# A fused mLSTM and two feed-forward layers: dense column sums on TensorE, and the first group's clipping on ScalarE

## The chip, the core and the metric

The kernel runs on one core of one Trainium2 chip. The metric is the device time of one execution in microseconds, lower is better. A core has five engines with a queue of instructions each, which run beside one another and wait for each other by semaphores: TensorE (PE; matmuls into PSUM, PEld its weight loads), VectorE (DVE), ScalarE (ACT), GpSimd (POOL) and SyncE (SP), which here issues most DMAs. Each engine takes its instructions strictly in the order in which they were written, so an instruction that waits holds up everything behind it on its engine.

## The reference

Three layers follow each other. An mLSTM attention over 4 batches, 8 heads and 768 steps gives 3072 tokens of 320 features. A dense feed-forward layer with 2048 hidden features follows, and then a routed one with 8 experts. The middle layer is the one that the change touches:

```python
def _moe_ref(x, w_in, w_out):                 # x: 3072 x 320, w_in: 320 x 2048, w_out: 2048 x 320
    h = x @ w_in
    g = np.where(h >= 1, h, np.where(h <= -1, 0.0, (h + 1) ** 2 / 4))
    return g @ w_out

def _moe2_ref(x, w_gate, w1, w2):             # shortened
    logits = x @ w_gate                       # 8 experts, each takes 384 tokens, best logits first
    ...
    out[mask] = np.maximum(x[mask] @ w1[e], 0) @ w2[e]
```

## The kernel before

**Tiling.** The 3072 tokens make 8 groups of 384 (three chunks of 128). For each group the dense layer runs over 16 feature tiles of 128 hidden features. One feature tile is an up step (`ff_up`, line 783: 8 matmuls of 384 columns into one PSUM tile `ph`), an activation, and a down step (`ff_down`, line 845: 3 matmuls of 328 columns for each of three chunks into `po`). Every 32-bit factor is split into a high part in the format `fp32r` and a low part, the rest, so an up step has high times high, high times low and low times high products, and a down step three. The 328 columns are the 320 of `w_out` and 8 more, `w_out` times the gate weights, so that the routed layer's logits come out of the same matmuls.

**The activation.** On the scaled up result, ScalarE makes `u = relu(h/2 + 1/2)` (line 793) and `r = relu(h - 1)` (line 795), VectorE clips `u` to at most 1 (line 797), ScalarE squares it (line 798), VectorE forms `r - 0.25 + u` (line 799), ScalarE writes its high part `gh` (line 810) and VectorE its low part `gl` (line 811). What comes out is g - 0.25, not g. So 0.25 times the column sums of `w_out` has to be added to every down result: that row is `crow`. GpSimd adds up the 16 weight tiles in `crow`, one add of 128 x 328 for each (line 753); then `col_sums` multiplies it by a 128 x 128 tile full of 0.25 (`quart`), which sums over the partitions and gives the same row to each of them (line 757), and ScalarE writes it back (line 759). Lines 834 and 865 add it.

**The weights.** In group 0 the weights of the 16 feature tiles come in as 64-bit numbers and are decoded (`load_w`): one step on ScalarE (line 714), three on VectorE (lines 716, 717 and 719, all in the buffer `ws`), then high parts on ScalarE (lines 725 and 748) and low parts on GpSimd (726 and 750). TensorE transposes the tile (`pw`, line 733) and multiplies it by the gate weights (`pg`, line 744). So up step f of group 0 needs decoded tile f. Groups 1 to 7 use the same weights from SBUF.

**Attention beside it.** While the dense layer of group g runs, the attention chunks of group g + 1 are worked on between its steps: loads, a scan (line 489), scores (`ps`, lines 558 and 562), state (`pu`, `um`, lines 576 and 579), outputs (`py`, lines 597 to 624), and the split of the result into `xh` and `xl` (lines 638 to 646). Their PSUM tiles come from a pool `psa` of three.

**What sets the order.** All steps are given to a planner (`Plan`) with an estimated duration, the tiles read and written, and a due time, which runs backwards from the steps that need them. `order` places the steps one by one: on each engine, of those that could start at the earliest time, the one due first. `issue` writes the instructions in that order. Where TensorE has an early gap, filler matmuls on `quart` stand in it (`pdm`, line 347). The planner's estimates only set the order; on the chip every engine runs through its queue as its semaphores allow.

## Time and profile before

| | us |
|---|---|
| median of 3 runs (lowest, highest) | 859.82 (858.64, 862.1) |
| the profiled execution's own time | 859.59 |
| its span, first to last instruction | 857.9 |
| TensorE busy (share of the span) | 804.5 (94%) |
| VectorE busy | 636.1 (74%) |
| ScalarE busy | 460.6 (54%) |
| GpSimd busy | 246.7 (29%) |

The shares are means over stages. Group 0 of the dense layer begins with its first up step at 53.20 us and ends near 158 us, groups 1 to 7 follow, and behind them the routing and the experts. Three views are used below. The view by stage has for each stretch its length and the busy time of PE, PEld, DVE, ACT and POOL with the count of instructions, then the granted clock of TensorE (1.00 is full), the DMA engines' busy share and GB/s. The view of waits names an instruction and what ended its engine's idle time before it. The timeline has a start, a duration and an instruction, written as line, operation and out<-in by the names in the program. Matmuls are pipelined, so the durations of neighbours overlap; how fast they run is read from one start to the next.

### The profile page before, as it was taken

The page shows a single profiled execution, that of the slowest core. Times are in us where ns is not written, and L with a number is a line of the kernel's source. Part 1 is how long each engine was busy: PE and PEld are TensorE (multiplying, and loading weights), DVE is VectorE, ACT ScalarE, POOL GpSimd, SP SyncE. Part 2 cuts the span into 40 slices and gives each one's busy share as a digit, 9 for nine tenths or more (in the row PEclk, how much of TensorE's full clock was granted, in tenths as well). Part 3 has the DMA queues.
Part 4 walks back from the last instruction along what each step waited for, and adds up shares of the span by engine and source line. Part 5 has one row for each costly group of instructions (what it writes and reads, how often), then busy time and mean ns, then how long its engine had stood idle before and what let it go on. Part 6 is the DMA issues. An engine that isn't in the chain of part 4 may idle for free. (4 is left out here: it accounts for less than half of the span.)

```text
span 857.9 us, 15542 instructions
## 1 busy us (share of the span) xinstructions
PE 804.5 (94%) x5459; PEld 751.3 (88%) x5459; DVE 636.1 (74%) x1549; ACT 460.6 (54%) x986; POOL 246.7 (29%) x332
## 2 busy tenths in 40 slices
PE   9988898999999999999999999998979799999896
PEld 7877787899999999999999998887959598898896
DVE  6889978676886886877787666747667787897461
ACT  4456666757656657657566667902233433442551
POOL 4666756220221320120221235002030321322411
PEclk9998899999999999999999999999979699999999
DMA  9775554031432423441430000005042442452630
GB/s 198 195 194 142 144 149 97 24 76 45 97 68 57 94 64 70 96 98 22 105 70 16 24 2 24 1 8 160 26 156 59 139 143 89 133 159 79 202 106 24
DMA packets 167846, 78.36 MB, mean 91 GB/s; under 512 B 105432, under 2 KB 164056, under 8 KB 167768
## 3 DMA queue, kind: packets, MB, share of 16 engines
q1 hardware_dynamic: 165464, 69.50, 31.7%
q0 software_dynamic: 2304, 7.87, 2.8%
q8 instruction: 43, 0.70, 0.3%
q14 instruction: 35, 0.29, 0.1%
HBM read 69.28 MB, written 8.06 MB: 90 GB/s over the span
## 5 line engine op out<-in xcount | busy, mean ns | idle before, releaser
L783 PE MATMUL ph<-xh,wi 128*128 128x384 f32 x768 | 180.4, 345 | 0.6 <-ACT r L795 0.4
L845 PE MATMUL po<-wo,gh 128*128 128x328 f32 (+1 forms) x690 | 162.5, 319 | 0.8 <-ACT gh L810 0.4
L783 PEld LDWEIGHTS ph<-xh,wi 128*128 128x128 f32 x768 | 134.9, 191 | 3.0 <-ACT r L795 2.0
L845 PEld LDWEIGHTS po<-wo,gh 128*128 128x128 f32 x690 | 120.4, 192 | 2.9 <-ACT gh L810 2.3
L845 PE MATMUL po<-wo,gl 128*128 128x328 f32 (+1 forms) x345 | 109.8, 318 | 4.5 <-DVE gl L811 4.4
L799 DVE SCALAR_TENSOR_TENSOR r<-r,u 128x384 f32<-128x384 f32 x128 | 77.9, 609 | 34.1 <-ACT u L798 33.2
L783 PE MATMUL pf<-xh_e,w1t 128*128 128x384 f32 x384 | 98.8, 363 | 0.1
L793 ACT ACTIVATE u<-ph,half 128x384 f32<-128x384 f32 x128 | 74.2, 580 | 39.4 <-PE ph L783 38.6
L810 ACT ACTIVATE gh<-r 128x384 fp32r<-128x384 f32 x115 | 60.3, 524 | 64.6 <-DVE r L799 64.6
L1311 ACT ACTIVATE hh<-pf 128x384 fp32r<-128x384 f32 x64 | 31.5, 492 | 114.2 <-PE pf L783 85.9
L811 DVE TENSOR_TENSOR gl<-r,gh 128x384 fp32r<-128x384 f32 x115 | 73.1, 636 | 25.0 <-ACT gh L810 24.3
L845 PE MATMUL pe<-w2t,hh 128*128 128x320 f32 x384 | 89.4, 319 | 0.0
L798 ACT ACTIVATE u<-u 128x384 f32<-128x384 f32 x128 | 67.3, 526 | 26.7 <-DVE u L797 26.0
L783 PE MATMUL ph<-xl,wi 128*128 128x384 f32 x256 | 76.2, 350 | 0.0
L795 ACT ACTIVATE r<-ph,none 128x384 f32<-128x384 f32 x128 | 74.4, 581 | 0.5 <-DVE st L811 0.5
L783 PEld LDWEIGHTS pf<-xh_e,w1t 128*128 128x128 f32 x384 | 71.2, 201 | 1.7 <-ACT xh_e L640 0.6
L845 PEld LDWEIGHTS po<-wo,gl 128*128 128x128 f32 x345 | 65.9, 191 | 6.6 <-DVE gl L811 6.6
L797 DVE TENSOR_SCALAR u<-u 128x384 f32<-128x384 f32 x128 | 54.4, 425 | 16.7 <-ACT u L793 15.8
L845 PEld LDWEIGHTS pe<-w2t,hh 128*128 128x128 f32 x384 | 65.3, 192 | 0.2
L845 PE MATMUL pe<-w2t,hl 128*128 128x320 f32 x192 | 59.8, 311 | 0.0
L1312 DVE SCALAR_TENSOR_TENSOR hl<-pf,hh 128x384 fp32r<-128x384 f32 x64 | 35.5, 555 | 28.6 <-ACT hh L1311 27.9
L489 DVE TENSOR_TENSOR_SCAN g<-g,identr 128x1024 f32<-128x1024 f32 x22 | 53.6, 2437 | 0.2
(219 smaller groups left out, 1634.3 us busy)
## 6 DMA issues: line engine op xcount, KB each, us to landing
g<-fz_d SPq DMA_DIRECT2D x22, 512.0 KB
r<-in_moe_w_dram SPq DMA_DIRECT2D x32, 320.0 KB
r<-in_moe_w_dram SPq DMA_DIRECT2D x32, 256.0 KB
raw<-in_moe_w_out_dram SPq DMA_DIRECT2D x16, 320.0 KB
raw<-in_moe_w_in_dram SPq DMA_DIRECT2D x16, 256.0 KB
r<-in_moe_w_dram SPq DMA_DIRECT2D x64, 64.0 KB
qn<-in_q_dram SPq DMA_DIRECT2D x24, 160.0 KB
kn<-in_k_dram SPq DMA_DIRECT2D x24, 160.0 KB
```

The costliest lines, as they stand in the source:

```text
L489: add("V", 2.25, lambda: V.tensor_tensor_scan(hl(gt()), hl(gt()), hl(identr()), 0.0, op0=OP.mult, op1=OP.add), r=[identr], w=[gt])
L783: T.matmul(ps()[:, :TG], wsrc(m, j), x()[:, j, :], start=(i == 0), stop=(i == len(ops) - 1))
L793: add("A", cost_act(TG, True), lambda: A.activation(u(), ps()[:, :TG], AF.Relu, bias=half(), scale=0.5 / 256), r=[ps, half], w=[u])
L795: add("A", cost_act(TG, True), lambda: A.activation(r(), ps()[:, :TG], AF.Relu, bias=none(), scale=1.0 / 256), r=[ps, none], w=[r])
L797: add("V", cost_v(TG, True), lambda: V.tensor_scalar(u(), u(), 1.0, None, op0=OP.min), w=[u])
L798: add("A", cost_act(TG, psum=False), lambda: A.activation(u(), u(), AF.Square), w=[u])
L799: add("V", cost_v(TG), lambda: V.scalar_tensor_tensor(r(), r(), -0.25, u(), op0=OP.add, op1=OP.add), r=[u], w=[r])
L810: add("A", cost_act(TG, psum=False), lambda: A.activation(hv(), r(), AF.Copy), r=[r], w=[hk])
L811: add("V", cost_v(TG), lambda: V.tensor_tensor(lv(), r(), hv().bitcast(F32), op=OP.subtract), r=[r, hk], w=[lk])
L845: T.matmul(po()[:, :n], a()[:, cs], w(), start=(first and m == 0), stop=(last and m == 2))
L1311: add("A", cost_act(TG), lambda ps=ps, hh=hh: A.activation(hh(), ps()[:, :TG], AF.Relu), r=[ps], w=[hh])
L1312: add("V", cost_v(TG), lambda ps=ps, hh=hh, hl=hl: V.scalar_tensor_tensor(hl(), ps()[:, :TG], 0.0, hh().bitcast(F32), op0=OP.max, op1=OP.s ...
```

## The change

Three edits. The 16 adds into `crow` on GpSimd go, and `col_sums` instead multiplies the tile of 0.25 (a copy `quart_r` in the format `fp32r`, made by VectorE) by the high and low parts of all 16 down weight tiles, 32 matmuls of 328 columns that accumulate in one PSUM tile of the pool `psa`; the planner gets them in 8 steps of four. In group 0 alone, the clipping of `u` on VectorE is replaced: ScalarE makes `relu(1 - u)` and then squares `1 - ` that, which is min(u, 1) squared. In the other groups the clipping stays.

```diff
--- before.py
+++ after.py
@@ -329,6 +329,7 @@
     none = ct([P, 1], F32, "none")
     crow = ct([P, DO], F32, "crow")
     quart = ct([P, P], F32R, "quart")
+    quart_r = ct([P, P], F32R, "quart_r")
     wg = ct([P, 3, NE], F32, "wg")
 
     def g_ident():
@@ -338,6 +339,7 @@
     add("G", 2.2, g_ident, w=[identr])
     if 20:
         add("V", 0.2, lambda: V.memset(quart().bitcast(F32), 0.25), w=[quart])
+        add("V", 0.16, lambda: V.tensor_copy(quart_r(), quart().bitcast(F32)), r=[quart], w=[quart_r])
         pdm = pl.tile(at(ps_o), [P, 512], F32, "pso", GC, "pdm")
 
         def filler(t):
@@ -403,8 +405,7 @@
         G.tensor_tensor(pair(), identr()[:2 * NE, 0, :NE], identr()[:2 * NE, 0, NE:2 * NE], op=OP.add)
         G.memset(half(), 0.5)
         G.memset(none(), -1.0)
-        G.memset(crow(), 0.0)
-    add("G", 1.4, g_small, r=[identr], w=[hm, half, none, crow, pair])
+    add("G", 1.4, g_small, r=[identr], w=[hm, half, none, pair])
 
     NR = 3
     KG = 2
@@ -750,12 +751,16 @@
         add("G", 1.2, lambda: G.tensor_tensor(
             w2_()[:, 1, f2, :], ws()[:, 3 * P:], w2_().bitcast(F32)[:, 0, f2, :], op=OP.subtract),
             r=[ws, (ws, "g"), (w2_, f, 0)], w=[(w2_, f, 1)])
-        add("G", 1.2, lambda: G.tensor_tensor(crow(), crow(), ws()[:, 3 * P:], op=OP.add), r=[ws, (ws, "g")], w=[crow])
 
     def col_sums():
         ps = pst("pcol")
-        add("T", 0.56, lambda: T.matmul(ps()[:, :DO], quart().bitcast(F32), crow(), start=True, stop=True),
-            r=[quart, crow], w=[ps])
+        for lo in range(0, NF, 2):
+            def f(lo=lo):
+                for f in (lo, lo + 1):
+                    for m in range(2):
+                        T.matmul(ps()[:, :DO], quart_r(), wo(f)()[:, m, f % (NF // 2), :],
+                                 start=(f == 0 and m == 0), stop=(f == NF - 1 and m == 1))
+            add("T", 4 * (DO * 0.000445 + 0.003), f, r=[quart_r] + wo_k(lo) + wo_k(lo + 1), w=[ps])
         add("A", cost_act(DO), lambda: A.activation(crow(), ps()[:, :DO], AF.Copy, scale=1.0 / 256), r=[ps], w=[crow])
 
     def spare():
@@ -794,8 +799,12 @@
             r=[ps, half], w=[u])
         add("A", cost_act(TG, True), lambda: A.activation(r(), ps()[:, :TG], AF.Relu, bias=none(), scale=1.0 / 256),
             r=[ps, none], w=[r])
-        add("V", cost_v(TG, True), lambda: V.tensor_scalar(u(), u(), 1.0, None, op0=OP.min), w=[u])
-        add("A", cost_act(TG, psum=False), lambda: A.activation(u(), u(), AF.Square), w=[u])
+        if g == 0:
+            add("A", cost_act(TG, psum=False), lambda: A.activation(u(), u(), AF.Relu, bias=1.0, scale=-1.0), w=[u])
+            add("A", cost_act(TG, psum=False), lambda: A.activation(u(), u(), AF.Square, bias=1.0, scale=-1.0), w=[u])
+        else:
+            add("V", cost_v(TG, True), lambda: V.tensor_scalar(u(), u(), 1.0, None, op0=OP.min), w=[u])
+            add("A", cost_act(TG, psum=False), lambda: A.activation(u(), u(), AF.Square), w=[u])
         add("V", cost_v(TG), lambda: V.scalar_tensor_tensor(r(), r(), -0.25, u(), op0=OP.add, op1=OP.add), r=[u], w=[r])
         k = f - (NF - ND) - 3
         if g < NG - 1 or k < 0:
```

The planner orders group 0 anew; from the fourth up step of group 1 on, every engine has the same instructions in the same order as before. Three places of the new order, on TensorE and VectorE. The first is TensorE's queue around up step 9 of group 0 (`ph_9`), before:

```order
L733 MATMUL pw_1257<-identr,ws_1175 128x128 x2
L733 MATMUL pw_1257<-identr,ws_1175 64x128
L499 MATMUL pq_1266<-identr,qn_94 120x128 x3
L845 MATMUL po_0_696<-wo_1076,gh_8_1252 128x328 x2
L845 MATMUL po_0_696<-wo_1076,gl_8_1255 128x328
L845 MATMUL po_1_702<-wo_1076,gh_8_1252 128x328 x2
L845 MATMUL po_1_702<-wo_1076,gl_8_1255 128x328
L845 MATMUL po_2_737<-wo_1076,gh_8_1252 128x328 x2
L845 MATMUL po_2_737<-wo_1076,gl_8_1255 128x328
L744 MATMUL pg_1290<-wg,wt_1270 128x8 x3
L783 MATMUL ph_9_1296<-xh_403,wi_1018 128x384 x3
```

and now (`pw` and `pg` are the transposed weight tile and its gate product, `pu` and `ps` belong to an attention chunk, `po` is a down step):

```order
L734 MATMUL pw_1261<-identr,ws_1185 128x128 x2
L734 MATMUL pw_1261<-identr,ws_1185 64x128
L577 MATMUL pu_1268<-v_0_117,kn_112 120x126 x3
L761 MATMUL pcol<-wo_425,quart_r 128x328 x4
L559 MATMUL ps_0_1285<-qm_1137,kT_1220 128x384
L761 MATMUL pcol<-wo_425,quart_r 128x328 x4
L745 MATMUL pg_1296<-wg,wt_1288 128x8 x3
L788 MATMUL ph_9_1301<-xh_403,wi_1042 128x384 x3
L788 MATMUL ph_9_1301<-xl_431,wi_1042 128x384 x2
L788 MATMUL ph_9_1301<-xh_403,wi_1042 128x384 x3
L639 MATMUL px_1319<-identr,x_615 128x128 x3
L854 MATMUL po_0_695<-wo_1074,gh_8_1308 128x328 x2
```

Two steps of four column-sum matmuls have come in between, ahead of `pg`, and the up step stands ahead of the down step that it used to follow. Four matmuls follow the down step, four more the next `ps`, and then eight in a row stand ahead of the next down step:

```order
L854 MATMUL po_2_711<-wo_1074,gl_8_1316 128x328
L761 MATMUL pcol<-wo_425,quart_r 128x328 x4
L559 MATMUL ps_1_1351<-qm_1137,kT_1220 128x384
L761 MATMUL pcol<-wo_425,quart_r 128x328 x4
L734 MATMUL pw_1364<-identr,ws_1266 128x128 x2
L734 MATMUL pw_1364<-identr,ws_1266 64x128
L761 MATMUL pcol<-wo_1074,quart_r 128x328 x8
L854 MATMUL po_0_695<-wo_1074,gh_9_1368 128x328 x2
L854 MATMUL po_0_695<-wo_1074,gl_9_1378 128x328
```

The last four of the 32 stand in group 1, in front of its fourth up step.

The second place is VectorE's queue where the tenth weight tile is decoded (`ws_1031` before, `ws_1032` now), whose last step, line 719 before and 720 now, TensorE awaits. Before:

```order
L811 TENSOR_TENSOR gl_5_1064<-r_5_1009,gh_5_1051 128x384
L717 SCALAR_TENSOR_TENSOR ws_1031<-raw_928,ws_1031 128x704
L489 SCALAR_TENSOR_TENSOR g_980<-g_980,identr 128x1024
L797 TENSOR_SCALAR u_6_1088<-u_6_1088 128x384
L719 SCALAR_TENSOR_TENSOR ws_1031<-raw_928,ws_1031 128x704
L716 TENSOR_SCALAR ws_1110<-ws_1110 128x704
L799 SCALAR_TENSOR_TENSOR r_6_1093<-r_6_1093,u_6_1088 128x384
```

and now:

```order
L717 TENSOR_SCALAR ws_1032<-ws_1032 128x704
L808 SCALAR_TENSOR_TENSOR r_5_1021<-r_5_1021,u_5_1016 128x384
L718 SCALAR_TENSOR_TENSOR ws_1032<-raw_928,ws_1032 128x704
L820 TENSOR_TENSOR gl_5_1065<-r_5_1021,gh_5_1056 128x384
L720 SCALAR_TENSOR_TENSOR ws_1032<-raw_928,ws_1032 128x704
L563 TENSOR_TENSOR g_515<-ps_0_1054,g_515 128x384
L580 TENSOR_TENSOR um_1091<-pu_1044,hm 120x378
```

The clipping of `u_6` is gone from between the decode steps, and the scan of an attention chunk (`g_980`) stands elsewhere; one tile's activation steps have moved in instead.

The third place is VectorE's queue ahead of group 0's first up step, where the third weight tile is decoded (`ws_439` before, `ws_438` now). Before:

```order
L717 SCALAR_TENSOR_TENSOR ws_439<-raw_382,ws_439 128x704
L644 TENSOR_TENSOR xl_432<-px_464,xh_403 128x2x128
L719 SCALAR_TENSOR_TENSOR ws_439<-raw_382,ws_439 128x704
L616 TENSOR_SCALAR rc_506<-py_477 128x8
L646 TENSOR_TENSOR xh_403<-px_464,xh_403 64x128
L617 TENSOR_TENSOR rc_506<-rc_506,py_477 128x8
L530 TENSOR_TENSOR qe_520<-pq_498,eat_118 120x384
L618 RECIPROCAL rc_506<-rc_506 128x8
L489 SCALAR_TENSOR_TENSOR g_434<-g_434,identr 128x1024
L624 TENSOR_TENSOR x_241<-py_477,x_241 128x320
```

and now:

```order
L718 SCALAR_TENSOR_TENSOR ws_438<-raw_382,ws_438 128x704
L490 SCALAR_TENSOR_TENSOR g_433<-g_433,identr 128x1024
L617 TENSOR_SCALAR rc_519<-py_478 128x8
L645 TENSOR_TENSOR xl_431<-px_469,xh_403 128x2x128
L618 TENSOR_TENSOR rc_519<-rc_519,py_478 128x8
L720 SCALAR_TENSOR_TENSOR ws_438<-raw_382,ws_438 128x704
L619 RECIPROCAL rc_519<-rc_519 128x8
L647 TENSOR_TENSOR xh_403<-px_469,xh_403 64x128
L717 TENSOR_SCALAR ws_517<-ws_517 128x704
L531 TENSOR_TENSOR qe_544<-pq_495,eat_120 120x384
L625 TENSOR_TENSOR x_241<-py_478,x_241 128x320
```

The scan of `g_434` has moved from behind the reciprocal of `rc` to ahead of the last decode step of this tile (line 719 before, 720 now).

## Rows read from the trace of the kernel before

**Rows 1.** Busy us by engine and stage: group 0, then the groups behind it.

```profile
53.00:158.00 105.00, 90.86 (x544) 82.87 (x544) 91.02 (x130) 67.81 (x164) 70.56 (x58) 0.92 0.52 131
158.00:497.00 339.00, 336.57 (x2225) 327.67 (x2224) 257.62 (x533) 218.72 (x467) 63.47 (x86) 1.00 0.29 65
```

**Rows 2.** Waits of TensorE between 53 and 158 us: us in total, times, longest us.

```profile
PE pw L733 <- DVE ws L719: 4.7, 2, 3.4
PE po L845 <- DVE gl L811: 4.4, 3, 2.8
PE pg L744 <- ACT wt L736: 2.6, 4, 1.0
```

**Rows 3.** Timeline of TensorE: start us, us, instructions [idle before, us <-what ended it].

```profile
65.07 0.90 PE L597 MATMUL py<-um,qe 120*128 120x126 f32 x6 [1.25 <-DVE um L579]
78.63 0.52 PE L733 MATMUL pw<-identr,ws 128*128 128x128 f32 x3 [1.33 <-DVE ws L719]
102.66 0.87 PE L733 MATMUL pw<-identr,ws 128*128 128x128 f32 x3 [3.36 <-DVE ws L719]
132.34 0.64 PE L845 MATMUL po<-wo,gl 128*128 128x328 f32 x1 [2.79 <-DVE gl L811]
153.40 0.42 PE L845 MATMUL po<-wo,gl 128*128 128x328 f32 x1 [1.00 <-DVE gl L811]
```

**Rows 4.** The same view as group 1: four stretches of low granted clock (after POOL).

```profile
67.00:71.00 4.00, 4.00 (x17) 3.99 (x16) 3.90 (x5) 2.64 (x7) 3.72 (x4) 0.57 0.49 95
81.00:85.00 4.00, 4.00 (x16) 4.00 (x16) 2.59 (x5) 1.70 (x5) 2.51 (x2) 0.57 0.43 128
101.00:109.00 8.00, 5.86 (x22) 5.39 (x23) 6.39 (x10) 4.72 (x12) 4.45 (x5) 0.57 0.49 144
132.00:136.00 4.00, 3.66 (x15) 3.58 (x16) 4.00 (x8) 1.58 (x4) 1.13 (x1) 0.57 0.29 85
```

**Rows 5.** Timeline of VectorE and GpSimd ahead of the wait that ended at 102.66 us.

```profile
97.86 2.97 DVE L489 TENSOR_TENSOR_SCAN g<-g,identr 128x1024 f32<-128x1024 f32 x1
98.64 2.86 POOL L753 TENSOR_TENSOR crow<-crow,ws 128x328 f32<-128x328 f32 x1
100.75 0.96 DVE L797 TENSOR_SCALAR u<-u 128x384 f32<-128x384 f32 x1
```

**Rows 6.** Instructions by line, 53 to 158 us: busy us, mean ns | idle before.

```profile
L797 DVE TENSOR_SCALAR u<-u 128x384 f32<-128x384 f32 x16 | 11.4, 713 | 6.0 <-ACT u L793 5.9
L799 DVE SCALAR_TENSOR_TENSOR r<-r,u 128x384 f32<-128x384 f32 x15 | 11.1, 739 | 2.1 <-ACT u L798 1.8
L753 POOL TENSOR_TENSOR crow<-crow,ws 128x328 f32<-128x328 f32 x13 | 16.4, 1264 | 15.1 <-ACT ws L746 15.1
L798 ACT ACTIVATE u<-u 128x384 f32<-128x384 f32 x15 | 7.8, 522 | 8.2 <-DVE u L797 8.0
```

**Rows 7.** Lines 797 and 799 from 158 to 497 us: ns min/median/max, first and last start.

```profile
L797 DVE TENSOR_SCALAR u<-u x88: 334/355/959, 160.4 to 494.1; 128x384 f32<-128x384 f32 x88
L799 DVE SCALAR_TENSOR_TENSOR r<-r,u x89: 531/558/1193, 158.8 to 495.3; 128x384 f32<-128x384 f32 x89
```

**Rows 8.** Timeline of VectorE: four clippings of group 0.

```profile
62.42 0.98 DVE L797 TENSOR_SCALAR u<-u 128x384 f32<-128x384 f32 x1
115.32 1.03 DVE L797 TENSOR_SCALAR u<-u 128x384 f32<-128x384 f32 x1 [1.08 <-ACT u L793]
128.63 1.04 DVE L797 TENSOR_SCALAR u<-u 128x384 f32<-128x384 f32 x1
146.26 1.04 DVE L797 TENSOR_SCALAR u<-u 128x384 f32<-128x384 f32 x1
```

**Rows 9.** Timeline of TensorE: first of nine down matmuls, what follows them; the old sum.

```profile
90.51 0.47 PE L845 MATMUL po<-wo,gh 128*128 128x328 f32 x2
91.87 0.49 PE L733 MATMUL pw<-identr,ws 128*128 128x128 f32 x3
164.92 0.71 PE L757 MATMUL pcol<-crow,quart 128*128 128x328 f32 x2
```

## The prediction

> **What bounds the kernel now.** I read the busy time by stage first, then what TensorE waited for in the one stage that the change touches, then the long waits one by one, then the engine that TensorE waited for. In the order of instructions everything behind the third up step of group 1 stands as before; so the change is decided in group 0, from its first up step at 53 us to about 158 us. In [rows 1] the reader is to see that these 105 us hold 90.86 us of TensorE, 91.02 of VectorE, 67.81 of ScalarE and 70.56 of GpSimd, while the next 339 us hold 336.57 of TensorE: there TensorE is full, and what group 0 saves or loses moves all that follows by the same amount.
>
> TensorE is idle for 105 - 90.86 = 14.1 us of the stage. In [rows 2] the reader is to see for whom: 4.7 us for the decoding of the weights on VectorE (line 719) and 4.4 for the low part of the activation (line 811), 2.6 for ScalarE. [Rows 3] are five of the long waits, with 1.25 for VectorE's line 579; the third wait for line 811 is 4.4 - 2.79 - 1.00 = 0.6. So VectorE accounts for 4.7 + 4.4 + 1.25 = 10.4, all else for 3.7. Behind the waits stands a second cost: in four stretches the granted clock averages 0.57 [rows 4], mostly the lower of its two levels (1.2 instead of 2.4 GHz), and each stretch begins during such a wait or within 3 us behind one. TensorE is busy 4.00 + 4.00 + 5.86 + 3.66 = 17.52 us in them; at full clock it would be 57% of that, so the clock costs 7.5 us. TensorE's real work in the stage is then 90.86 - 7.5 = 83.4 us.
>
> Why VectorE is late is shown in [rows 5]: the scan takes 2.97 us, beside it the GpSimd add into crow 2.86, and the clipping (line 797), which starts as the scan ends, needs 0.96 and ends 0.2 us after that add. Only then does the decode step start that TensorE awaits.
>
> **The change part by part.** *Clipping.* VectorE loses 16 instructions of 0.713 us, 11.4 us of its 91.0 [rows 6]. They are not 11.4 us of work: in the next groups, where GpSimd is busy 63 of 339 us [rows 1], the same instruction has a median of 0.355 [rows 7], so about 16 x 0.358 = 5.7 us are waiting. I take off each long wait the clipping that stands in VectorE's queue shortly ahead of it, at its contended time [rows 3, 5, 8]: 3.36 loses 0.96, 2.79 loses the 1.04 at 128.63 us, 1.33 and 1.25 each lose the 0.98 at 62.42 us, from which VectorE runs on unbroken, 0.6 and 1.00 go (1.03 at 115.32 us and 1.04 at 146.26 us). That leaves 2.4 + 1.75 + 0.35 + 0.3 = 4.8 of 10.4 us. Bounds: 10.4 (nothing arrives) and 0.
>
> The Trainium skill, "SBUF — State Buffer", section "SBUF: two separate sides", says that VectorE and GpSimd share one port pair as an exclusive lock, held for a whole instruction, also against VectorE instructions with two SBUF inputs. The trace agrees: the two-input line 799 too averages 0.739 us here against a median of 0.558 in the next groups [rows 6, 7]. It speaks against counting 0.96 to 1.04 each: where the GpSimd instruction stays, the next two-input instruction takes over the wait. That is a rival below.
>
> *ScalarE* gets the 16 instructions, at 0.522 us each [rows 6] 8.4 us, to 76 of the stage; it has 105 - 67.8 = 37 us free, which hides them unless they lie on the path. They do lie in the chain up step, ScalarE, VectorE, ScalarE, VectorE, down step, where they take the clipping's place. Bounds: 16 x (0.522 - 0.713) = -3.1 and +8.4; I take +1.0, nearer the lower end, because TensorE waits for ScalarE far less than for VectorE now.
>
> The Trainium skill, "ScalarE: Activation LUTs", section "Rules for kernel authors", says to put min and relu on VectorE, not on ScalarE. By the row of the later groups this holds (0.522 against 0.355, +2.7 us over 16), by the row of this stage it does not (0.522 against 0.713, -3.1 us); this stage decides.
>
> *Column sums.* GpSimd loses 13 adds of 1.264 us in the stage, 16.4 of its 70.6 us [rows 6]. I count nothing for it beyond the clippings' share, since TensorE waits for nothing that GpSimd writes; what VectorE may gain more is bounded by line 799 and the like, 15 x (0.739 - 0.558) = 2.7 us for one such line, and by 0 below. TensorE gains 32 matmuls of 328 columns. Nine such take 91.87 - 90.51 = 1.36 us [rows 9], 0.151 each. Four stand in group 1, 0.6 us, in place of the old sum, whose two matmuls took about as long (0.71 with the last one's tail [rows 9]): nothing on balance. 28 stand between up steps 8 and 12 of group 0: 4.2 us. In the order they lie where TensorE waits today: ahead of a `pg` step (TensorE's 2.6 us for ScalarE are all ahead of `pg`) and, eight in a row, ahead of the tenth down step. Bounds: 0 (all in gaps) and 4.2; I take half, 2.1. If their cover goes, because VectorE is no longer late, they cost all 4.2, but then the gaps are gone too. The eight need the low part of a weight that GpSimd makes; if it is late, the tenth down step and all of TensorE's queue wait behind them.
>
> *Clock.* Two stretches, 67 to 71 and 81 to 85 us, follow waits that I expect to shrink to 0.3 us (1.25, 1.33): 8.0 x 0.43 = 3.4 us back. The other two keep 9.52 x 0.43 = 4.1. Bounds: 0 and 7.5.
>
> *Ahead of 53 us* VectorE's order changes too, a scan moves ahead of pieces of the weights' decoding. One scan is 2.97 us [rows 5], so the bounds are -3 and +3; I take 0, since the same instructions stand there. The copy of `quart` is one small VectorE instruction while the gates load, and hidden by that.
>
> **Sum.** 83.4 work + 2.1 column sums + 3.7 other waits + 1.0 longer chain + 4.8 waits for VectorE + 4.1 clock = 99.1 us for the stage instead of 105: 5.9 less. The profiled execution took 859.59 us (the span of 857.9 and 1.7 around it); 859.6 - 5.9 = 853.7. The median of the runs is 859.82, 0.2 above it, which I leave out.
>
> **Rivals.** *The wait is passed on.* VectorE, blocked behind a GpSimd instruction, starts its next two-input instruction no earlier, and a clipping is worth 0.355, not 0.96 to 1.04 (the rule on the port pair works so). Then the waits keep 3.0 + 2.4 + 1.0 + 0.9 + 0.25 + 0.65 = 8.2 instead of 4.8, and the clock stretch behind the 1.33 stays (1.7): 5.1 more, 858.8. For it: 5.7 of the 11.4 us are waiting. Against it: in [rows 5] the blocking instruction is itself one of those removed.
>
> *More than forecast.* Waits for VectorE and lower clock both vanish and the column sums fill gaps: 859.6 - 10.4 - 7.5 + 1.0 = 842.7. For it: VectorE falls from 91 to about 80 us. Against it: with an order that is fixed ahead some waits stay even where VectorE has room (1.00 at 153.40 us).
>
> *ScalarE takes VectorE's place (slower).* TensorE waits for the last squaring instead of for line 719, all 16 new instructions lie on the path, no wait or clock is given back, and half of the column sums add: 859.6 + 8.4 + 2.1 = 870.1. It decides as soon as TensorE's wait for ScalarE per tile (2.6 / 16 = 0.16 now) grows by more than (5.6 + 3.4) / 16 = 0.56, what the waits for VectorE and the clock give back. For it: three ScalarE instructions now follow each other on one chain. Against it: 37 us free on ScalarE.
>
> That the change doesn't do what it says I leave out: the order has neither the adds nor the clippings of group 0.
>
> **How the numbers follow.** Forecast (847 to 855.3) 0.50; more than forecast 0.12; wait passed on (855.3 to 862) 0.24; ScalarE the bound 0.14. About 0.5%, 4.3 us, is what a measurement of this kernel can tell from no change: faster is below 855.5, slower above 864.1. Faster: 0.50 + 0.12 and 0.04 of the third = 0.66; same: 0.20; slower: 0.14. The range from 844 to 863 leaves out about 0.06 below and 0.13 above.
>
> **What would show it.** Right: group 1 begins about 6 us earlier, TensorE's waits for lines 719 and 811 are halved, fewer than four stretches of low clock stand in the stage, ScalarE is near 76 us and VectorE near 80, and TensorE's share behind the stage is the same. Passed on: line 799 and the decode steps longer than now, with as many waits. Wrong: new waits of TensorE for the squaring or ahead of the column sums, low clock in as many places, or a start of group 0 more than 1 us later than 53.

## The result and the profile after

| | before | after |
|---|---|---|
| median us (lowest, highest) | 860.96 (858.64, 862.74), 6 runs | 849.06 (847.64, 850.92), 6 runs |
| ratio to before, 95% interval | | 0.9864 (0.9844 to 0.9883) |
| the profiled execution's own time | 859.59 | 848.75 |
| its span | 857.9 | 847.0 |
| VectorE / ScalarE / GpSimd busy | 636.1 / 460.6 / 246.7 | 626.9 / 463.9 / 221.8 |

The change makes the kernel 11.9 us faster, by the profiled executions 10.8. The forecast was 853.7: the direction is right, the size about half of what came. In the code of after, some lines have moved: 718 and 720 are the old 717 and 719 (decoding), 734 the old 733 (`pw`), 745 the old 744 (`pg`), 808 and 820 the old 799 and 811, 854 the old 845 (down steps).

The first view is the busy time by stage. Group 0 is now cut at the same two instructions in both kernels: the first up step, and the first up step behind the last column-sum matmul, which is the fourth up step of group 1. Before:

```profile
53.20:165.22 112.02, 97.88 (x587) 89.80 (x586) 94.76 (x138) 73.07 (x175) 70.36 (x58) 0.92 0.48 123
165.22:497.00 331.78, 329.35 (x2181) 320.53 (x2180) 253.69 (x525) 213.46 (x456) 63.47 (x86) 1.00 0.29 66
```

After, the same stretches, and last the only stretch of low granted clock that is left in group 0; it answers to [rows 1, 4]:

```profile
49.77:154.35 104.58, 96.42 (x614) 88.96 (x613) 84.85 (x121) 77.31 (x191) 49.10 (x44) 0.98 0.52 132
154.35:486.00 331.65, 329.29 (x2183) 320.71 (x2182) 253.81 (x525) 213.30 (x457) 63.78 (x86) 1.00 0.29 66
84.80:88.20 3.40, 3.40 (x14) 3.40 (x13) 2.73 (x5) 3.40 (x11) 1.35 (x1) 0.50 0.11 13
```

The groups behind take 331.65 us instead of 331.78: nothing happens there. Group 1 reaches the same instruction 10.87 us earlier (165.22 - 154.35), which is the whole difference of the spans (10.9). Of it 3.43 us are there when group 0 begins (53.20 - 49.77), and 7.44 arise in group 0 (112.02 - 104.58).

The 7.44 have three parts. TensorE's idle time falls from 112.02 - 97.88 = 14.1 to 104.58 - 96.42 = 8.2 us: 6.0 less. The low clock cost 7.5 us [rows 4] and now costs half of 3.40, 1.7: 5.8 less. Without that cost TensorE's work was 97.88 - 7.5 = 90.4 and is 96.42 - 1.7 = 94.7: 4.3 more, which are the new matmuls. 6.0 + 5.8 - 4.3 = 7.5.

TensorE's waits in group 0 after the change answer to [rows 2]: us in total, times, longest us.

```profile
PE pg L745 <- ACT wt L737: 3.6, 4, 1.8
PE px L639 <- DVE x L625: 1.5, 1, 1.5
PE px L639 <- DVE g L563: 1.1, 2, 0.8
PE po L854 <- DVE gl L820: 0.8, 1, 0.8
PE py L598 <- DVE g L563: 0.5, 1, 0.5
PE pw L734 <- DVE ws L720: 0.3, 1, 0.3
```

The waits for the decoding and for the activation's low part, 4.7 and 4.4 us in [rows 2], are 0.3 and 0.8. New ones for VectorE, of 1.5, 1.1 and 0.5 us, have come in the attention chunks; all waits for VectorE together are 4.2 us, where 10.4 were. The wait for ScalarE ahead of `pg` went from 2.6 to 3.6.

The instructions of the same stretch by line answer to [rows 6]: busy us, mean ns, idle before.

```profile
L718 DVE SCALAR_TENSOR_TENSOR ws<-raw,ws 128x704 uint32<-128x704 uint32 x12 | 16.0, 1335 | 0.0
L720 DVE SCALAR_TENSOR_TENSOR ws<-raw,ws 128x704 uint32<-128x704 uint32 x12 | 13.4, 1113 | 0.0
L808 DVE SCALAR_TENSOR_TENSOR r<-r,u 128x384 f32<-128x384 f32 x18 | 13.0, 721 | 2.7 <-ACT u L804 1.8 <-ACT u L807 0.9
L804 ACT ACTIVATE u<-u 128x384 f32<-128x384 f32 x16 | 8.4, 526 | 0.0
```

The same view of before has the two decode lines at 1200 and 984 ns. They have become slower (13.4 - 11.8 and 16.0 - 14.4, 3.2 us together), and line 808 is hardly faster, 721 ns against 739 in [rows 6]. That the clippings' wait has been passed on to them is not shown: with the clippings put back in this same order (below) the two decode lines take 1376 and 1054 ns, together as long. On ScalarE each of the 16 added instructions takes 0.526 us, as [rows 6] had it, but ScalarE's busy time in the stage grew by 4.2 us only (73.07 to 77.31): where one ScalarE instruction follows another without a wait, their records overlap.

**Ahead of group 0.** Timelines of VectorE, GpSimd and TensorE around 43 us (start, duration, instruction, idle before), put together. Before:

```profile
42.96 3.06 DVE L489 TENSOR_TENSOR_SCAN g<-g,identr 128x1024 f32<-128x1024 f32 x1
43.82 2.71 POOL L622 TENSOR_TENSOR x<-x,rc 128x320 f32<-128x320 f32 x1
46.56 0.49 DVE L624 TENSOR_TENSOR x<-py,x 128x320 f32<-128x320 f32 x1 [0.55 <-POOL x L622]
47.20 1.59 PE L576 MATMUL pu<-v,kn 128*120 128x126 f32 x6 [2.44 <-DVE x L624]
```

After:

```profile
39.25 2.97 DVE L490 TENSOR_TENSOR_SCAN g<-g,identr 128x1024 f32<-128x1024 f32 x1
43.70 0.72 POOL L623 TENSOR_TENSOR x<-x,rc 128x320 f32<-128x320 f32 x1 [0.94 <-DVE rc L619]
45.31 0.48 DVE L625 TENSOR_TENSOR x<-py,x 128x320 f32<-128x320 f32 x1
45.45 0.91 PE L577 MATMUL pu<-v,kn 128*120 128x126 f32 x6 [0.43 <-DVE qe L531]
```

Beside the scan the GpSimd product of `x` takes 2.71 us and TensorE waits 2.44 us for what follows from it; with the scan planned 3.7 us earlier the same product takes 0.72 us and that wait is gone. With the adds left out and the old order kept, the scan stays where it was, and so do the product (2.70 us) and the wait (2.36 us): the scan's place is what made them. The prediction had seen that the scan moves, and had put no gain on it.

That wait is not the whole of the 3.43 us. The stage ahead of group 0, before and after:

```profile
0.00:53.20 53.20, 47.88 (x320) 41.68 (x321) 40.17 (x61) 24.16 (x52) 29.95 (x52) 0.94 0.83 192
0.00:49.77 49.77, 45.64 (x327) 40.70 (x327) 40.49 (x62) 24.42 (x52) 26.08 (x48) 1.00 0.88 206
```

TensorE's idle time falls only from 5.3 to 4.1 us. The rest is the granted clock, 0.94 on the mean before and 1.00 after: before, one of the stretches of low clock begins at 46.9 us, at the end of that wait. And three of GpSimd's 16 adds stand ahead of group 0 (the first at 32.72 us): leaving the adds out in the old order, with the scan in its old place, brings the start of group 0 from 53.20 to 51.24 us. How much of the 3.43 us belongs to the scan and how much to the adds is not shown.

### The profile page after: what moved, and what is told of

It is laid out like the page before. It is cut to its first block, busy times and chain, and to the rows that moved or that the text cites. A ratio compares the mean times of both kernels' runs of the same rounds, so it can differ in the third digit from the quotient of the medians.

```text
span 847.0 us, 15577 instructions
## 1 busy us (share of the span) xinstructions
PE 800.3 (94%) x5493; PEld 748.6 (88%) x5493; DVE 626.9 (74%) x1534; ACT 463.9 (55%) x1002; POOL 221.8 (26%) x315
## 5 line engine op out<-in xcount | busy, mean ns | idle before, releaser
L788 PE MATMUL ph<-xh,wi 128*128 128x384 f32 x768 | 178.5, 343 | 0.7 <-ACT r L800 0.4
L854 PE MATMUL po<-wo,gh 128*128 128x328 f32 (+1 forms) x690 | 160.3, 316 | 0.2
L807 ACT ACTIVATE u<-u 128x384 f32<-128x384 f32 x112 | 58.9, 526 | 18.6 <-DVE u L806 18.1
L490 DVE TENSOR_TENSOR_SCAN g<-g,identr 128x1024 f32<-128x1024 f32 x22 | 51.8, 2353 | 1.3 <-DMA g<-fz_d 1.2
L806 DVE TENSOR_SCALAR u<-u 128x384 f32<-128x384 f32 x112 | 43.0, 384 | 11.4 <-ACT u L798 10.5
```

The lines of the kernel that those rows point to most:

```text
L490: add("V", 2.25, lambda: V.tensor_tensor_scan(hl(gt()), hl(gt()), hl(identr()), 0.0, op0=OP.mult, op1=OP.add), r=[identr], w=[gt])
L788: T.matmul(ps()[:, :TG], wsrc(m, j), x()[:, j, :], start=(i == 0), stop=(i == len(ops) - 1))
L806: add("V", cost_v(TG, True), lambda: V.tensor_scalar(u(), u(), 1.0, None, op0=OP.min), w=[u])
L807: add("A", cost_act(TG, psum=False), lambda: A.activation(u(), u(), AF.Square), w=[u])
L854: T.matmul(po()[:, :n], a()[:, cs], w(), start=(first and m == 0), stop=(last and m == 2))
```

## The experiments

All ratios are to the runs of the kernel before on the same chip, with a 95% interval; the changed kernel's is 0.9864 (0.9844 to 0.9883). The experiments were measured in three sets, in which the kernel before had medians of 862.64 us (the two halves, and either part left out), 862.23 us (both parts left out, parts put back, 30 matmuls left out) and 860.74 us (the rest), against 860.96 us beside the changed kernel. So kernels of different sets are compared by their ratios, not by their microseconds.

### The two halves of the change, each planned anew

Column sums on TensorE, clipping left on VectorE (and again with more runs):

```diff
-        add("G", 1.2, lambda: G.tensor_tensor(crow(), crow(), ws()[:, 3 * P:], op=OP.add), r=[ws, (ws, "g")], w=[crow])
...
-        add("T", 0.56, lambda: T.matmul(ps()[:, :DO], quart().bitcast(F32), crow(), start=True, stop=True),
-            r=[quart, crow], w=[ps])
...
+                        T.matmul(ps()[:, :DO], quart_r(), wo(f)()[:, m, f % (NF // 2), :],
+                                 start=(f == 0 and m == 0), stop=(f == NF - 1 and m == 1))
```

> The column sums on TensorE as changed, the clipping left on VectorE in all groups; the planner makes a new order. The kernel before takes 861 us, the changed one 849. Theory (VectorE's late work is what TensorE waited for, and the clippings with their waiting are most of it): the adds alone give a third, 857 us, with VectorE's clipping in group 0 still at about 0.6 us. Rival, the wait is passed on (what blocks VectorE is the GpSimd instruction, so taking that one away is what counts): 853 us, clippings near 0.4 us. Rival, the new order alone decides: anything from 849 to 861, with no relation to VectorE's busy time in the stage.

> Column sums on TensorE alone, clipping on VectorE, planned anew: the same kernel as measured at 848.1 (4 runs), with more runs. Theory (the clipping's move is worth nothing beside the column sums): 847-851, within 0.3% of the changed kernel's 849.1. Rival (the move is worth something and the first measurement was lucky): 852-855.

Measured: 848.13 us, ratio 0.9854 (0.981 to 0.9897), and 845.35 us, 0.9832 (0.9803 to 0.986). The column sums alone are at least as fast as the whole change. The clipping's move adds nothing to them; that it costs a few us is possible, but the intervals overlap and the two kernels did not run side by side. The second trace (stage, then VectorE's clipping and decoding by line in it):

```profile
49.41:152.48 103.07, 94.11 (x599) 86.96 (x598) 87.41 (x134) 71.93 (x173) 46.67 (x42) 0.98 0.51 133
```

```profile
L802 DVE TENSOR_SCALAR u<-u 128x384 f32<-128x384 f32 x18 | 7.9, 437 | 5.1 <-ACT u L798 5.1
L718 DVE SCALAR_TENSOR_TENSOR ws<-raw,ws 128x704 uint32<-128x704 uint32 x12 | 14.7, 1228 | 0.0
```

With the adds gone these 18 clippings (two of group 1 among them) take 0.437 us each on VectorE. Between the same cuts they took 0.674 us before, and 0.525 with the adds gone and the old order kept.

The clipping moved to ScalarE, the adds left on GpSimd:

```diff
-        add("V", cost_v(TG, True), lambda: V.tensor_scalar(u(), u(), 1.0, None, op0=OP.min), w=[u])
+        if g == 0:
+            add("A", cost_act(TG, psum=False), lambda: A.activation(u(), u(), AF.Relu, bias=1.0, scale=-1.0), w=[u])
+            add("A", cost_act(TG, psum=False), lambda: A.activation(u(), u(), AF.Square, bias=1.0, scale=-1.0), w=[u])
...
```

> The clipping of group 0 on ScalarE as changed, the column sums left on GpSimd; the planner makes a new order. Theory (the clippings are most of it): 853 us, TensorE's waits for lines 719 and 811 (9.1 us before) fall to under 4. Rival, the wait is passed on: 858 us, and VectorE's two-input decode steps grow from 1.20 and 0.98 us by what the clippings waited. Rival, ScalarE's longer chain costs: 862 us, with new waits of TensorE for ScalarE.

Measured: 854.35 us, 0.9909 (0.9878 to 0.994). So either half gains; but the halves don't add up (0.9% and 1.5 to 1.7%, together 1.4%): both take load from the same place, VectorE beside GpSimd. The trace of this half stands between two of the theories: TensorE's waits for the decoding and for the activation's low part are 6.6 us (9.1 before, under 4 expected), and the decode steps have grown to 1.35 and 1.12 us. As this kernel is planned anew, its gain can lie in the clipping's move or in its order; no run separates them.

### Parts left out, everything else in the old order

The clippings of group 0 left out:

```diff
-        add("V", cost_v(TG, True), lambda: V.tensor_scalar(u(), u(), 1.0, None, op0=OP.min), w=[u])
+        add("V", cost_v(TG, True), lambda: g and V.tensor_scalar(u(), u(), 1.0, None, op0=OP.min), w=[u])
```

> The kernel before in its own order, instruction for instruction, but the 16 clippings of group 0 are left out and nothing stands in their place (the activation of group 0 is then not clipped). Theory: 853 us, VectorE 10 us less busy in the stage. Rival, the wait is passed on: 857 us or more, since only 16 x 0.35 us are work and the blocked time goes to the next two-input instruction. Rival, the new order is what gained: 859 us or more.

Measured: 859.24 us, 0.9977 (0.9951 to 1.0002): no gain that can be told from none, though 16 VectorE instructions are gone. The lines of this trace in group 0 show where it went (GpSimd's low part of a weight, ScalarE's copy that starts the next weight):

```profile
L750 POOL TENSOR_TENSOR wo<-ws,wo 128x328 fp32r<-128x328 f32 x13 | 19.3, 1483 | 0.0
L714 ACT ACTIVATE ws<-raw 128x704 f32<-128x704 f32 x11 | 9.3, 850 | 7.9 <-POOL wo L750 5.5 <-POOL crow L753 2.3
```

The same lines of before:

```profile
L750 POOL TENSOR_TENSOR wo<-ws,wo 128x328 fp32r<-128x328 f32 x13 | 16.9, 1297 | 0.1
L714 ACT ACTIVATE ws<-raw 128x704 f32<-128x704 f32 x11 | 9.3, 846 | 3.2 <-POOL crow L753 2.3 <-POOL wo L750 0.8
```

And TensorE's waits with the clippings left out:

```profile
PE pg L744 <- ACT wt L736: 4.9, 4, 3.1
PE pw L733 <- ACT ws L714: 3.1, 1, 3.1
PE po L845 <- DVE gl L811: 2.3, 2, 1.7
```

VectorE is earlier with its other instructions: TensorE no longer waits for line 719 (4.7 us before), and for line 811 it waits 2.3 us instead of 4.4. But now GpSimd is what is late: its subtraction takes 1.48 instead of 1.30 us, the buffer that it holds comes free later, ScalarE waits 7.9 us instead of 3.2 to start the next weight, and TensorE waits 3.1 us for that in one place and for ScalarE 2.3 us more than before in another. A part of the wait is passed on, round a loop of four engines, and a part to VectorE's decode steps, in the same order as before:

```profile
L717 DVE SCALAR_TENSOR_TENSOR ws<-raw,ws 128x704 uint32<-128x704 uint32 x12 | 15.5, 1296 | 0.0
L719 DVE SCALAR_TENSOR_TENSOR ws<-raw,ws 128x704 uint32<-128x704 uint32 x12 | 13.1, 1093 | 0.1
```

Not all of it is passed on in this trace: group 0, cut as above, takes 107.4 us instead of 112.0. The rest of the span, with the same instructions, takes 697.1 us instead of 692.7, and such differences come between traces without any change (last section). So the clippings may be worth something in the old order too, up to the 0.5% that the interval allows.

The adds left out, clippings kept; and both left out:

```diff
-        add("G", 1.2, lambda: G.tensor_tensor(crow(), crow(), ws()[:, 3 * P:], op=OP.add), r=[ws, (ws, "g")], w=[crow])
+        add("G", 1.2, lambda: None, r=[ws, (ws, "g")], w=[crow])
```

> The kernel before in its own order, but GpSimd's 16 adds into crow are left out (the constant row is then zero). Theory: 858 us, since TensorE waits for nothing that GpSimd writes and only part of VectorE's blocked time goes. Rival, the wait is passed on (the GpSimd instruction is what blocks): 853 us, the clippings near 0.4 us, the scan near 2.3. Rival, the new order is what gained: 860 us.

> The kernel before in its own order, with both the 16 clippings of group 0 and GpSimd's 16 adds left out, nothing in their place. Leaving out the adds alone gave -7 us, the clippings alone -2. Theory now (the GpSimd instruction is what blocks; the clippings' wait is passed on): about 853 us, -8 to -9, and still three or more stretches of low clock; what the changed kernel (849) has beyond it comes from its order and from column sums that stand in TensorE's gaps. Rival (with the adds gone the clippings' time counts in full): 847 us.

Measured: 856.22 us, 0.9917 (0.9885 to 0.9949), and 854.41 us, 0.9896 (0.9846 to 0.9946). Taking 16 adds from GpSimd, for which TensorE never waited, gains 0.8%; leaving out the clippings as well gains nothing that can be told apart from it. With the adds alone left out, TensorE's waits for VectorE in group 0 are 6.8 us instead of 10.4, and ScalarE no longer waits for the buffer that GpSimd held (0.2 us instead of 3.2):

```profile
PE pw L733 <- DVE ws L719: 3.6, 2, 2.7
PE po L845 <- DVE gl L811: 2.6, 2, 2.2
PE py L597 <- DVE um L579: 0.6, 1, 0.6
L714 ACT ACTIVATE ws<-raw 128x704 f32<-128x704 f32 x11 | 9.3, 843 | 0.2 <-POOL wo L750 0.2
```

Group 0 between the two cuts, with the clippings out, the adds out, and both out:

```profile
52.34:159.77 107.43, 95.92 (x588) 88.80 (x586) 87.44 (x122) 72.76 (x175) 70.81 (x58) 0.94 0.51 129
51.24:157.05 105.81, 96.32 (x588) 88.42 (x586) 88.39 (x136) 73.46 (x175) 50.50 (x44) 0.94 0.50 128
52.18:155.81 103.63, 95.54 (x587) 88.95 (x586) 82.92 (x121) 72.47 (x175) 53.10 (x45) 0.93 0.51 132
```

TensorE's idle time, 14.1 us before, is 11.5, 9.5 and 8.1 us; in the changed kernel it is 8.2.

### Parts put back, in the new order

The 16 adds put back on GpSimd, into a tile that nobody reads; the clipping put back on VectorE in the place of the ScalarE instruction:

```diff
+            G.tensor_tensor(junk[:, :], junk[:, :], ws()[:, 3 * P:], op=OP.add)
```

```diff
-            add("A", cost_act(TG, psum=False), lambda: A.activation(u(), u(), AF.Relu, bias=1.0, scale=-1.0), w=[u])
-            add("A", cost_act(TG, psum=False), lambda: A.activation(u(), u(), AF.Square, bias=1.0, scale=-1.0), w=[u])
+            add("A", cost_act(TG, psum=False), lambda: V.tensor_scalar(u(), u(), 1.0, None, op0=OP.min), w=[u])
+            add("A", cost_act(TG, psum=False), lambda: A.activation(u(), u(), AF.Square), w=[u])
```

> The changed kernel in its own order, with 16 GpSimd adds of 128 x 328 put back, each ahead of the low part of a down weight, into a tile that nobody reads. Theory (the GpSimd instruction blocks VectorE and holds the decode buffer): 855 us, +6, VectorE's two-input lines longer and ScalarE's first decode step waiting for the buffer. Rival (the new order is what gained): 850 us, +1 at most.

> The changed kernel in its own order, with the clipping of group 0 back on VectorE where the added ScalarE instruction stood. Theory now (the clippings are worth little): 849 to 850 us, ScalarE 8 us less busy in the stage, VectorE 7 more. The theory of the prediction (each takes VectorE about 0.7 us that TensorE waits for): 854 us. Rival, ScalarE is the bound of the changed kernel: 846 us.

Measured: 856.74 us, 0.9932 (0.9902 to 0.9962), so the adds cost 0.7%, some 6 us, in the new order too, and ScalarE waits for GpSimd's buffer again (no wait at this line in the changed kernel):

```profile
L717 ACT ACTIVATE ws<-raw 128x704 f32<-128x704 f32 x12 | 10.2, 854 | 2.9 <-POOL wo L755 2.6
```

The second measured 854.63 us, 0.9886 (0.9834 to 0.9939). It is inconclusive: its runs lie from 850.33 to 863.83, and its interval holds the changed kernel's ratio. With the first half measured above, planned anew, the clipping on VectorE is no loss.

### The column sums taken away, replaced, added

30 of the 32 matmuls left out of the changed kernel:

```diff
+                        if (f, m) in ((0, 0), (NF - 1, 1)):
                           T.matmul(ps()[:, :DO], quart_r(), wo(f)()[:, m, f % (NF // 2), :],
```

> The changed kernel in its own order with 30 of its 32 column-sum matmuls left out (the constant row is then wrong). 30 x 0.151 = 4.5 us of TensorE's work go. As predicted, half of them in gaps: 847 us. Rival, all on the path: 844.5. Rival, they keep TensorE busy in gaps and the clock up: 849 us or slower, with more stretches of low clock than the one that the changed kernel has in group 0.

Measured: 855.1 us, 0.9907 (0.9879 to 0.9936): with 30 x 0.151 = 4.5 us less work for TensorE the kernel is 0.43% slower by the ratios, 3.7 us. (The medians are 6 us apart, but come from different sets.) To see where, group 0 is cut at three gate products (`pg`) that both kernels have. The changed kernel, with all column sums:

```profile
103.66:121.72 18.06, 16.24 (x101) 14.33 (x99) 17.09 (x22) 10.86 (x27) 11.48 (x9) 1.00 0.53 145
121.72:127.46 5.74, 5.74 (x46) 5.61 (x45) 2.88 (x6) 4.12 (x11) 2.71 (x4) 1.00 0.41 126
127.46:153.76 26.30, 25.38 (x160) 24.39 (x158) 19.19 (x29) 21.46 (x52) 10.59 (x9) 1.00 0.20 45
```

With two of them:

```profile
104.29:122.30 18.01, 13.23 (x77) 10.78 (x76) 17.04 (x22) 10.85 (x27) 11.44 (x9) 1.00 0.54 144
122.30:131.18 8.88, 8.88 (x47) 8.52 (x46) 4.34 (x7) 4.62 (x11) 3.06 (x4) 0.62 0.28 83
131.18:157.46 26.28, 24.74 (x156) 23.76 (x154) 18.35 (x28) 21.09 (x51) 10.09 (x9) 1.00 0.21 46
```

In the first stretch 24 matmuls fewer (by the counts) and 3.0 us less work change the time by 0.05 us (18.06 and 18.01): all of it lay in gaps. In the second, which has the same work in both, the granted clock falls to 0.62 on the mean where TensorE was less busy just before, and the stretch takes 8.88 instead of 5.74 us: 3.1 lost. The third is equal. Those 3.1 us are shown. Over the whole of group 0 the two traces differ by 3.7 us (108.2 and 104.6): ahead of the first cut, where TensorE has the same instructions in both, the kernel with two is another 1.0 us slower, and the three matmuls that it lacks in group 1 give 0.45 back. The effect does not rest on these traces alone: the granted clock over the whole execution was 0.961 to 0.970 in the seven runs with two column-sum matmuls and 0.972 to 0.976 in the six with all.

This kernel also answers the rival that the new order alone gained. It has neither adds nor clippings of group 0, and hardly any column sums, as the kernel with both parts left out, but stands in the new order (and has ScalarE's 16 more instructions): 0.9907 against 0.9896 (0.9846 to 0.9946) in the old. The new order by itself is not shown to gain.

The same matmuls at the same places, but all reading one weight that has been ready for long:

```diff
-                        T.matmul(ps()[:, :DO], quart_r(), wo(f)()[:, m, f % (NF // 2), :],
+                        T.matmul(ps()[:, :DO], quart_r(), wo(0)()[:, 0, 0, :],
```

> The changed kernel, its 32 column-sum matmuls at the same places but all reading the first weight's high part (ready long ago), so the sum is another and TensorE waits for no low part from GpSimd there. Theory (the matmuls help only because TensorE is busy in gaps and its granted clock then falls less often): as the changed kernel, 849 +-2. Rival (their waits for the weights' parts set the pace, or reading them costs time): with neither, away from 849 by 3 us or more, to 845 if the waits cost, to 855 if the pace helps.

Measured: 847.35 us, 0.9846 (0.9819 to 0.9873), as the changed kernel. The three stretches:

```profile
104.25:122.29 18.04, 16.23 (x100) 14.31 (x99) 17.07 (x22) 10.86 (x27) 11.45 (x9) 1.00 0.57 150
122.29:128.06 5.77, 5.77 (x47) 5.64 (x45) 2.88 (x6) 4.12 (x11) 2.72 (x4) 1.00 0.42 128
128.06:154.35 26.29, 25.35 (x159) 24.36 (x158) 19.18 (x29) 21.45 (x52) 10.61 (x9) 1.00 0.20 45
```

The clock stays at 1.00 whatever the matmuls compute, so neither their wait for the weights nor their data matters: that TensorE is busy in the gaps does. Over the whole execution its five runs had granted clocks of 0.971 to 0.976. With its interval the slowing by 30 matmuls fewer (0.9879 to 0.9936) does not overlap; with the changed kernel's it just does.

Such matmuls, read by nobody, in the old order and without the adds:

```diff
         def t_g():
+            for _ in range(2 if f else 0):
+                T.matmul(pg()[:, P:P + DO], wo(0)()[:, 0, 0, :P], wo(0)()[:, 0, 0, :], start=True, stop=True)
             for j in range(3):
...
-        add("G", 1.2, lambda: G.tensor_tensor(crow(), crow(), ws()[:, 3 * P:], op=OP.add), r=[ws, (ws, "g")], w=[crow])
+        add("G", 1.2, lambda: None, r=[ws, (ws, "g")], w=[crow])
```

> The kernel before with the GpSimd adds left out (the second output part of the dense sum is so missing; measured 856.2), and two matmuls of 328 columns that nobody reads ahead of each of 15 gate products of the weights' decoding, ahead of their wait: 30 more matmuls, 4.5 us of TensorE work at full clock. Theory (filled gaps keep the clock up whatever the work is): low-clock stretches in the stage from the first up step to the last weight fall from three to one or two and the time to 850-854 in spite of the added work. Rival (the gain of the changed kernel's column sums lies in their places in its own order): 856-860.5.

Measured: 850.62 us, 0.9877 (0.9849 to 0.9905), against 856.22, 0.9917 (0.9885 to 0.9949), without them. Between the first and the last gate product of group 0, without and with them:

```profile
54.44:140.84 86.40, 77.35 (x473) 70.45 (x471) 75.96 (x113) 60.75 (x146) 45.25 (x40) 0.92 0.56 145
```

```profile
57.34:142.05 84.71, 77.76 (x496) 71.75 (x495) 76.62 (x113) 60.51 (x146) 45.06 (x40) 0.96 0.58 151
```

23 matmuls more by the counts, and 1.7 us less. The ratios point the same way (3.4 us), though the intervals overlap, and the granted clock over the whole execution rises from 0.964 to 0.969 on the mean of all runs; with the pair above it is the second case of the same effect, in another order.

Sixteen more of them in the changed kernel, ahead of the waits of eight gate products:

```diff
         def t_g():
+            for _ in range(2 if 2 <= f < 10 else 0):
+                T.matmul(pg()[:, P:P + DO], quart_r(), wo(0)()[:, 0, 0, :], start=True, stop=True)
```

> The changed kernel with two more matmuls of 328 columns that nobody reads ahead of the wait of eight gate products, from the third weight to the tenth (up to the first column sums): 16 matmuls, 2.4 us of work. Theory of filled gaps: the one low stretch that is left, 3.4 us at 84.8 us, goes (-1.7) and half of the work lies in gaps: 848 +-1.5, at best a little faster than the changed kernel. Rival (TensorE has no more to win there, the work adds): 851.5.

Measured: 850.75 us, 0.9896 (0.9864 to 0.9927): no gain. A stretch of low clock still stands there, at 82.9 us. Filling a gap is thus no sure cure; here it won nothing. No kernel tried is shown to beat the column sums alone.

The clock records give two columns: the time at low granted clock within group 0 of the one trace of each kernel, and the granted clock over the whole execution for all runs of it.

| kernel | low clock in group 0, us | whole execution, all runs: mean (lowest to highest) |
|---|---|---|
| before | 17.1 | 0.962 (0.954 to 0.967) |
| clippings out (old order) | 13.6 | 0.960 (0.954 to 0.967) |
| adds out (old order) | 13.6 | 0.964 (0.961 to 0.967) |
| both out (old order) | 13.6 | 0.963 (0.959 to 0.966) |
| clipping moved alone | 13.6 | 0.966 (0.961 to 0.969) |
| changed, 30 column sums out | 13.6 | 0.966 (0.961 to 0.970) |
| changed, adds back | 13.6 | 0.968 (0.962 to 0.973) |
| changed, clipping back (its slowest run was traced) | 17.1 | 0.967 (0.958 to 0.972) |
| old order, adds out, matmuls added | 6.8 | 0.969 (0.966 to 0.973) |
| changed, 16 matmuls more | 6.8 | 0.973 (0.967 to 0.976) |
| changed, other data | 3.4 | 0.973 (0.971 to 0.976) |
| column sums alone (two traces) | 3.4, 3.4 | 0.975 (0.972 to 0.978) |
| changed | 3.4 | 0.974 (0.972 to 0.976) |

Only kernels with both, GpSimd freed of the adds and matmuls added to TensorE, are below 13.6, and all of those but the one with the clipping back are. In the first column a stretch can come or go from run to run (the two traces of the column sums alone have theirs at 111.8 and at 103.7 us); the second column, over all runs, puts the kernels in nearly the same order.

## Why the prediction was right in direction and wrong in size

- **Where it is decided: right.** Only the work up to group 1's first steps changed, and in the two traces all behind it moved by the same amount.
- **Waits for VectorE: the number right, its reason wrong.** 4.8 us were to be left of 10.4, and 4.2 are; that they agree is luck. For the prediction took the gain from the clippings and counted for GpSimd's adds "nothing for it beyond the clippings' share". The runs show that the adds count for themselves: without them and with the clippings kept, the whole gain is there (0.9854 and 0.9832), and in the old order they alone give 0.8% and take these waits to 6.8 us; putting them back costs 0.7%. The clippings left out alone, in the old order, gave 0.2%, which can't be told from none. GpSimd's adds are not waited for by TensorE, but they stand beside VectorE's instructions and in the loop that frees the weights' buffers. The rule on the shared port pair (the Trainium skill, "SBUF — State Buffer", section "SBUF: two separate sides") speaks of such a pair of instructions. The traces agree: with nothing but the adds taken away a clipping takes 0.525 us instead of 0.674, and with nothing but the clippings taken away the next two-input steps get longer (1.296 and 1.093 us instead of 1.200 and 0.984).
- **"The wait is passed on"**, given 0.24 at 858.8 us (0.1% less than before), is near to what the clippings left out alone did (0.2% less). In the changed kernel it is not shown: the two decode lines are 3.2 us longer, and stay so with the clippings put back.
- **ScalarE: right where it counts.** +1.0 us was taken for the longer chain; TensorE's wait for ScalarE ahead of `pg` grew from 2.6 to 3.6. Its busy time grew by 4.2 us, not by the 8.4 that led to 76.
- **Column sums: the step that failed.** "I take half, 2.1" as a cost. In the stretch with the most of them they cost 0.05 us, and by the clock they give 3.1 us back; without 30 of them the kernel is 3.7 us slower by the ratios: the sign was wrong. The bound "0 (all in gaps)" left out that work in a gap can pay.
- **Clock: undersized.** 4.1 of 7.5 us were to stay, 1.7 did. The two stretches counted as lasting, at 101 and 132 us [rows 4], are both gone, and the one that is left, at 84.8 us, stands near the one at 81 us that had been expected to go.
- **Group 0 in sum:** forecast 5.9, measured 7.4. Column sums and waits together were put at 2.1 + 3.7 + 1.0 + 4.8 = 11.6 and are 4.3 + 8.2 = 12.5, 0.9 worse; the clock is 2.4 better.
- **Ahead of group 0: missed.** Put at 0 between -3 and +3, "since the same instructions stand there"; it was -3.4, by the profiled executions the larger part of the error of 4.9 us (10.8 against 5.9). The same instructions do not stand there: three of the 16 adds did, and without the adds alone group 0 began 2.0 us earlier. And the scan that moved stood on a chain to TensorE, which the timeline of before shows (2.71 us for a GpSimd product that takes 0.72 without the scan beside it, and 2.44 us of TensorE waiting for it, with low clock behind). The prediction priced the scan by its length and not by what ran beside it.

## What to carry to other kernels

An instruction that nobody waits for can still be worth removing: price it by what runs slower beside it and by the buffers that its queue holds, not by the waits that name it. When work moves to a partly idle engine, find out whether it lands in gaps, and then look at the granted clock behind those gaps: here the added TensorE work kept the clock up and gave back more than it cost. When a planned order shifts a long VectorE instruction, look in the trace at what it stood beside, before and after.

## What the runs showed of the hardware that was not expected

- Less work on TensorE made the kernel slower: 30 matmuls fewer, a ratio of 0.9907 instead of 0.9864, with the next stretch at a granted clock of 0.62 instead of 1.00 and 8.88 us long instead of 5.74.
- A GpSimd product of 128x320 took 2.71 us beside a scan on VectorE and 0.72 without one; a clipping on VectorE took 0.674 us with GpSimd's adds there and 0.525 without them, in the same order.
- The time from the fourth up step of group 1 (the second cut) to the end of the span, in kernels with the same instructions there, was 692.7 us before and after, but 690.8 to 697.5 in the traces of the others, and up to 4.0 us apart within one set. A single profiled execution is thus uncertain by some 5 us behind the place of the edit; medians of one set and stretches cut at equal instructions were needed to tell the effects apart.
